# Reordering the first and last microseconds of an attention and feed-forward kernel: an earlier load, output tiles between the last contexts, adds on GpSimd, the last two tiles by halves

## The chip, the cores and the metric

The kernel runs on one core of one Trainium2 chip. The metric is the device time of one execution in microseconds (us), the median over several executions. PE is TensorE, DVE is VectorE, ACT is ScalarE, POOL is GpSimd, SP is SyncE, whose queue issues most DMAs. The *span* is the length of the profiled execution on the core, 1.75 to 1.92 us less than the device time.

## The reference

```python
# x: 2048 x 640; 32 heads of 192; only the last W = 512 keys are used
xn = layernorm(x)
q  = (xn @ wq) per head;  k, v = the last 512 rows of the caches
o  = softmax(q k^T * 192**-0.5) v          # per head
s  = concat(o) @ wo                        # 2048 x 640
g  = silu((silu(xn @ w_gate) * (xn @ w_up)) @ w_down)
return x + s * g
```

## The kernel before

The kernel handles the 2048 rows as 16 tiles of 128 rows. A context is one block of 512 rows (four tiles) of one pair of heads. It starts with the layernorm of the first four tiles and the gate and up products of the feed-forward part, then the rest of that part, then sixteen head pairs of attention. `sacc` collects x + g * (partial sum of `o @ wo`), `g2` holds g. In the last head pair the final sum of each tile is `PSUM * g2 + sacc`, a multiply on VectorE out of PSUM and an add of two SBUF tensors.

The start (cut):

```python
        load_x(0)
        load_x(1, nc.scalar)
        for cs in (slice(0, 1), slice(1, 3), slice(3, NC)):     # NC = 5 chunks of 128
            for eng, w_sb, w in ((nc.sync, wg_sb, B_w_gate), (nc.scalar, wu_sb, B_w_up)):
                ...                                             # a slice of each weight
        load_x(2)
        load_x(3)
        ...
        keep_warm(11)                       # matmuls on zeros
        def ready(t):                       # transposes on PE, then copies to SBUF
            ln_transpose(t)                 # five transposes
            rows = slice(t * P, (t + 1) * P)
            n = NC if t else 3
            nc.scalar.copy(xnT[:, 0:n, rows], tps[t][:, 0:n, :])
            if n < NC:
                nc.vector.tensor_copy(out=xnT[:, n:NC, rows], in_=tps[t][:, n:NC, :])
        ...
        keep_warm(3)
        for t in range(4):                  # t = 0 goes chunk by chunk, others bank by bank
            ...                             # after 3/5 of tile t's matmuls: normalise and ready(t + 1)
```

The end (cut). `pv` computes a half context, `wo_last` an output tile. Contexts 2 and 3 also take in the previous head pair there (`late`), so a tile of theirs has 12 matmuls and a tile of contexts 0 and 1 has 6. `sc_tile()` and `mm_tile()` give PSUM buffers out of two pools of two buffers each.

```python
    def wo_last(b, qt, eng):
        ...
        split = b == NB - 1 and qt == 3                # the last tile by halves
        sc = None if split else sc_tile()
        ...                                            # 6 or 12 matmuls
        if not split:
            nc.vector.tensor_tensor(s_f, sc, g2[t], ALU.mult)
            eng.tensor_tensor(ob, s_f, sacc[t], ALU.add)
        stores.append((t, ob))
    ...
    for b in range(NB - 1):
        for q2 in range(2):
            pv(i + b, q2)
    for q2 in range(2):
        wo_last(0, 2 * q2, G); wo_last(0, 2 * q2 + 1, G)
        pv(i + 3, q2)
    for qt in range(4):
        wo_last(1, qt, G)
        store(3)
        wo_last(2, qt, V if qt % 2 else G)
        transpose_o(i + 3, qt)                         # three PE transposes and a ScalarE copy
    for qt in range(4):
        store(2)
        wo_last(3, qt, V if qt else G)
    store(0)
```

The softmax here doesn't subtract the row's maximum and nothing guards it: scores larger than these inputs give would overflow.

## Time and profile before

| before | |
|---|---|
| time, median of 3 | 929.49 us (929.24 to 929.5) |
| span | 927.8 us |
| PE busy | 919.5 us (99%) |
| first matmul of the last head pair's `pv` ("the mark") | 890.91 us |
| last vector add ends | 924.97 us |

"The mark": between the start and this matmul PE never waits for long, so the time of the mark tells what the start cost, and times counted from it tell what the end cost.

From the page (engine, busy us, share, number of instructions; then the chain that ended last):

```profile
span 927.8 us, 18795 instructions
PE 919.5 (99%) x8009; PEld 578.7 (62%) x8025; DVE 579.4 (62%) x846; ACT 475.5 (51%) x849; POOL 65.0 (7%) x57
...
PE 98%; DMA 1%; DVE 1%; issue 0%; DVEq 0%
```

PE bounds everything but the edges. The start, from the timeline (start us, length us, engine, line, operation, output<-inputs, shapes, count, in brackets the engine's idle time before it and what ended it):

```profile
8.09 0.44 PE L262 MATMUL tp<-ident,xn 128*128 128x128 bf16 x5
...
8.37 0.22 PE L274 MATMUL sc<-xnT,wg_sb 128*128 128x128 bf16 x1
...
8.79 0.89 DVE L228 BATCH_NORM_STATS2 stats<-x_t 128x6 f32<-128x320 bf16 x2 [0.90 <-DMA x_t<-in_A_x_dram]
...
10.48 0.45 DVE L251 TENSOR_SCALAR xn<-x_t,mv,rstd 128x640 bf16<-128x640 bf16 x1
...
10.98 0.45 PE L262 MATMUL tp<-ident,xn 128*128 128x128 bf16 x5 [0.67 <-DVE xn L251]
```

VectorE waited for the third x tile until 8.79, so PE had its third tile to transpose only at 10.98, after 0.67 us of idle. The end, same view:

```profile
890.91 1.51 PE L461 MATMUL mm<-V_p,p_t 128*128 128x193 bf16 x16
...
907.57 0.33 PE L495 MATMUL trp<-ident,O_b 128*128 128x128 bf16 x3
...
907.73 0.98 PE L508 MATMUL sc<-wo_p,OT_b 128*128 128x320 bf16 x6
907.84 0.82 DVE L551 TENSOR_TENSOR s_f<-sc,g_76 128x640 f32<-128x640 f32 x1 [0.80 <-PE sc L508]
...
908.72 0.57 PE L508 MATMUL sc<-wo_p,OT_l 128*128 128x320 bf16 x3
...
916.26 1.55 POOL L554 TENSOR_TENSOR x_r<-s_f,sacc 128x640 bf16<-128x640 f32 x1
...
917.02 1.47 DVE L554 TENSOR_TENSOR ob<-s_f,sacc 128x640 bf16<-128x640 f32 x1
...
919.59 0.82 DVE L551 TENSOR_TENSOR s_f<-sc,g_76 128x640 f32<-128x640 f32 x1 [0.37 <-PE sc L508]
...
920.45 1.07 DVE L554 TENSOR_TENSOR ob<-s_f,sacc 128x640 bf16<-128x640 f32 x1
...
922.17 0.57 PE L508 MATMUL mm<-wo_p,OT_b 128*128 128x320 bf16 x3
...
924.48 0.49 DVE L549 TENSOR_TENSOR ob<-s_f,sacc 128x320 bf16<-128x320 f32 x1
```

A matmul of 320 columns takes PE 0.136 us in a row (12 in 1.63 us), but its printed length includes the modelled way through the array. So the six from 907.73 leave PE free at 908.55, and PE starts again at 908.72: 0.17 us lost. The same loss comes twice more, at 911.49 and 914.26.

### The profile page before, as it was taken

The page shows a single profiled execution, that of the slowest core. Times are in us where ns is not written, and L with a number is a line of the kernel's source. Part 1 is how long each engine was busy: PE and PEld are TensorE (multiplying, and loading weights), DVE is VectorE, ACT ScalarE, POOL GpSimd, SP SyncE. Part 2 cuts the span into 40 slices and gives each one's busy share as a digit, 9 for nine tenths or more (in the row PEclk, how much of TensorE's full clock was granted, in tenths as well). Part 3 has the DMA queues.
Part 4 walks back from the last instruction along what each step waited for, and adds up shares of the span by engine and source line. Part 5 has one row for each costly group of instructions (what it writes and reads, how often), then busy time and mean ns, then how long its engine had stood idle before and what let it go on. Part 6 is the DMA issues. An engine that isn't in the chain of part 4 may idle for free.

```text
span 927.8 us, 18795 instructions
## 1 busy us (share of the span) xinstructions
PE 919.5 (99%) x8009; PEld 578.7 (62%) x8025; DVE 579.4 (62%) x846; ACT 475.5 (51%) x849; POOL 65.0 (7%) x57
## 2 busy tenths in 40 slices
PE   9999999999999999999999999999999999999997
PEld 5455556574848474757575757575656666666675
DVE  6433331467676767676766666676767676767656
ACT  4222222556465656565655555555555555656561
POOL 0000000000000000000000000000000000003975
PEclk9999999999999999999999999999999999999999
DMA  9321510053525343433434342525252516262623
GB/s 300 69 54 34 114 35 1 1 86 79 102 62 92 72 86 77 79 86 74 90 72 92 65 99 59 105 53 111 41 122 40 124 35 129 35 144 59 147 59 107
DMA packets 240148, 76.34 MB, mean 82 GB/s; under 512 B 221120, under 2 KB 240064, under 8 KB 240064
## 3 DMA queue, kind: packets, MB, share of 16 engines
q1 hardware_dynamic: 239152, 74.40, 37.7%
q8 instruction: 63, 1.03, 0.5%
q10 hardware_dynamic: 912, 0.74, 0.3%
q14 instruction: 21, 0.17, 0.1%
HBM read 39.45 MB, written 2.62 MB: 45 GB/s over the span
## 4 chain that ended last, share of the span: by engine, by line
PE 98%; DMA 1%; DVE 1%; issue 0%; DVEq 0%
PE sc L508 22%; PE mm L425 22%; PE mm L461 18%; PE sc L439 18%; PE sc L274 10%; PE mm L296 6%; DMA x_t<-in_A_x_dram 1%; PE sc L461 1%; PE mm L274 0%; PE mm L309 0%; DVE s_f L551 0%; PE mm L439 0%; DVE stats L228 0%; DVE ob L549 0%; DVE s_f L548 0%
## 5 line engine op out<-in xcount | busy, mean ns | idle before, releaser
L443 ACT ACTIVATE p_t<-sc 128x1024 bf16<-128x1024 f32 x254 | 253.0, 1022 | 136.6 <-PE sc L439 136.6
L430 DVE TENSOR_REDUCE qT<-mm 128x512 bf16<-128x1024 f32 x189 | 231.2, 1223 | 104.0 <-PE mm L425 101.6
L478 ACT ACTIVATE O_b<-mm,r 128x192 bf16<-128x192 f32 x484 | 164.1, 421 | 175.5 <-DVE r L467 96.9
L425 PE MATMUL mm<-xnT,wq_p 64*128 64x512 bf16 x1890 | 235.0, 376 | 0.0
L508 PE MATMUL sc<-wo_p,OT_b 128*128 128x320 bf16 x1482 | 223.4, 299 | 0.0
L523 DVE TENSOR_TENSOR sacc<-sacc,sc 128x640 f32<-128x640 f32 x216 | 176.7, 821 | 60.9 <-PE sc L508 60.9
L439 PE MATMUL sc<-qT,khat 64*128 64x512 bf16 x1524 | 195.5, 376 | 0.0
L461 PE MATMUL mm<-V_p,p_t 128*128 128x193 bf16 x1984 | 185.8, 246 | 0.0
L461 PEld LDWEIGHTS <-p_t 128*128 128x128 bf16 x2048 | 173.0, 97 | 14.9 <-issue 7.0
L508 PEld LDWEIGHTS <-OT_b 128*128 128x128 bf16 x1488 | 143.5, 98 | 47.3
L425 PEld LDWEIGHTS <-wq_p 64*128 64x128 bf16 x1890 | 90.7, 94 | 112.4 <-issue 4.2
L439 PEld LDWEIGHTS <-khat 64*128 64x128 bf16 x1536 | 74.8, 94 | 91.0
L282 DVE TENSOR_TENSOR hT<-sc,sg 128x512 bf16<-128x512 f32 x46 | 31.6, 690 | 85.2 <-ACT sg L281 85.1
L526 POOL TENSOR_TENSOR sacc<-sacc,g_76 128x640 f32<-128x640 f32 x16 | 22.1, 1402 | 757.8 <-ACT O_b L478 757.8
L467 DVE RECIPROCAL r<-mm 128x4 f32<-128x4 f32 x124 | 22.7, 183 | 73.0 <-PE mm L461 68.9
L281 ACT ACTIVATE sg<-sc 128x512 bf16<-128x512 f32 x46 | 27.3, 596 | 72.4 <-PE sc L274 72.4
L274 PE MATMUL sc<-xnT,wg_sb 128*128 128x512 bf16 (+1 forms) x248 | 58.4, 353 | 0.7
L274 PE MATMUL sc<-xnT,wu_sb 128*128 128x512 bf16 (+1 forms) x259 | 59.0, 354 | 0.1
L296 PE MATMUL mm<-wd_sb,hT 128*128 128x320 bf16 x384 | 56.6, 299 | 0.0
L296 PEld LDWEIGHTS <-hT 128*128 128x128 bf16 x384 | 37.6, 98 | 18.9
L274 PEld LDWEIGHTS <-wu_sb 128*128 128x128 bf16 x285 | 26.3, 98 | 26.8 <-issue 0.2
L274 PEld LDWEIGHTS <-wg_sb 128*128 128x128 bf16 x285 | 26.4, 98 | 23.1 <-issue 0.2
(63 smaller groups left out, 250.9 us busy)
## 6 DMA issues: line engine op xcount, KB each, us to landing
wo_p<-in_A_wo_dram SPq DMA_DIRECT2D x16, 480.0 KB, 4.3
K_p<-in_A_k_cache_dram SPq DMA_DIRECT2D x32, 192.0 KB, 3.3
V_p<-in_A_v_cache_dram SPq DMA_DIRECT2D x32, 192.0 KB, 3.1
wq_p<-in_A_wq_dram SPq DMA_DIRECT2D x64, 80.0 KB, 3.1
wq_p<-in_A_wq_dram SPq DMA_DIRECT2D x16, 160.0 KB, 3.3
x_r<-in_A_x_dram SPq DMA_DIRECT2D x16, 160.0 KB, 3.6
x_t<-in_A_x_dram SPq DMA_DIRECT2D x14, 160.0 KB, 3.1
wd_sb<-in_B_w_down_dram SPq DMA_DIRECT2D x1, 1920.0 KB, 12.1
```

The costliest lines, as they stand in the source:

```text
L274: nc.tensor.matmul(out, w_sb[:, c, f * P : (f + 1) * P], xnT[:, c, qc], start=(c == 0), stop=(c == NC - 1),)
L281: nc.scalar.activation(sg[:], g, ACT.Silu)
L282: nc.vector.tensor_tensor(hTs[b][:, f, :], u, sg[:], ALU.mult)
L296: nc.tensor.matmul(dn[:, 0:HD], hTs[b][:, f, ti * P : (ti + 1) * P], wd_sb[:, f, cols], start=(f == 0), stop=(f == NF - 1),)
L425: nc.tensor.matmul(q_ps[:, h, :], pairs[pr]["wq"][r, c, j * P : (j + 1) * P], xnT[r, c, b * 512 : (b + 1) * 512], start=(c == 0), stop=(c ...
L430: nc.vector.reduce_sum(qTs[i][:, j, :], q_ps[:, :, :].rearrange("p h n -> p n h"), axis=AX.X)
L439: nc.tensor.matmul(sc[:, h, :], khat[r, j, ks], qT[r, j, :], start=(j == 0), stop=(j == 2))
L443: nc.scalar.activation(p_t[:, :, :], sc[:, :, :], ACT.Exp, scale=scale)
L461: nc.tensor.matmul(acc[:, k, h * 256 : h * 256 + Dh + 1], Ps[i][kc][:, h, qt * P : (qt + 1) * P], V_p[:, kc, h, 0 : Dh + 1], start=(kc == ...
L478: nc.scalar.activation(O_b[:, qt, h, :], a_k[:, h, 0:Dh], ACT.Copy, scale=r[:, k, h, :])
L508: nc.tensor.matmul(ps, OTs[i][:, 3 * qt + j, :], pairs[i // NB]["wo"][:, j, n * HD : (n + 1) * HD], start=(first and j == 0), stop=(end an ...
L523: nc.vector.tensor_tensor(s_t, s_t, sc[:, :, 0:HD], ALU.add)
```

## The change

Its intent: take the last PE transposes away (the DMA transposes instead), interleave output tiles with the last half contexts so that what they wait for is there, leave nearly all adds to GpSimd, and finish the last two tiles by halves with small stores. At the start, load the third x tile ahead of the last weight slices and let the first tile's chunks 0 and 1 go ahead. The diff, cut to its core:

```diff
         for cs in (slice(0, 1), slice(1, 3), slice(3, NC)):
+            if cs.stop == NC:
+                load_x(2)
             for eng, w_sb, w in ((nc.sync, wg_sb, B_w_gate), (nc.scalar, wu_sb, B_w_up)):
...
-        load_x(2)
         load_x(3)
...
-            n = NC if t else 3
+            n = NC if t else 2
...
-        ln_stats(1, lambda: ln_apply(0))
+        ln_stats(1, lambda: ln_apply(0, (slice(0, 2 * P), slice(2 * P, D))))
...
-        if (pr == last and b < NB - 1) or i == 0:
+        if pr == last or i == 0:
             nc.sync.dma_start_transpose(
...
+    def wo_end():
+        i = NS - 1
+        obs = [finp.tile([P, D], bf, name="ob", bufs=4) for k in range(2)]
+        s_fs = [finp.tile([P, 2, HD], f32, name="s_f", bufs=4) for k in range(2)]
+        for qt, n, mm in ((3, 0, mm_tile), (2, 0, mm_tile), (2, 1, sc_tile), (3, 1, sc_tile)):
+            t, cols = T - 4 + qt, slice(n * HD, (n + 1) * HD)
+            ob, s_f = obs[qt - 2], s_fs[qt - 2]
+            ps = mm()[:, 0, 0:HD]
+            wo_sum(ps, i, qt, n)
+            nc.vector.tensor_tensor(s_f[:, n, :], ps, g2[:, t, cols], ALU.mult)
+            nc.vector.tensor_tensor(ob[:, cols], s_f[:, n, :], sacc[:, t, cols], ALU.add)
+            (nc.scalar if n else nc.sync).dma_start(...)
...
+    work = [(0, 0), (0, 1), (1, 0), (1, 1), (2, 0)]
+    for b, q2 in work:
+        pv(i + b, q2)
+    for b, q2, more in ((0, 0, (2, 1)), (0, 1, (3, 0)), (1, 0, (3, 1)), (1, 1, None)):
+        for k in range(2):
+            wo_last(b, 2 * q2 + k, G)
+        if more:
+            pv(i + more[0], more[1])
+    for b in (2, 3):
+        for qt in range(4 if b < 3 else 2):
+            store(3)
+            wo_last(b, qt, V if (b, qt) == (3, 1) else G)
     store(0)
+    wo_end()
```

More of the change, by code (lines that the diff above doesn't have):

```diff
@@ L243, in ln_sqrt, with ln_apply @@
             )
-        def ln_apply(t):
+        def ln_apply(t, parts=(slice(0, D),)):
             b, ti = divmod(t, 4)
@@ L250, in ln_apply @@
                 nc.vector.reciprocal(rstd[:, t : t + 1], rstd[:, t : t + 1])
-            nc.vector.tensor_scalar(
-                xns[t][:], x_t.pop(t)[:], mv[:, ti, 0:1], rstd[:, ti : ti + 1],
-                op0=ALU.subtract, op1=ALU.mult,
-            )
+            for cols in parts:
+                nc.vector.tensor_scalar(
+                    xns[t][:, cols], x_t[t][:, cols], mv[:, ti, 0:1], rstd[:, ti : ti + 1],
+                    op0=ALU.subtract, op1=ALU.mult,
+                )
         tps = {}
@@ L453, in pv @@
         O_b, OT_b = Obs[i], OTs[i]
-        alone = i < 2 or (pr == last and b < NB - 1)
+        alone = i < 2 or (pr == last and 2 * b + q2 < 5)
         acc = sc_tile() if alone and q2 and b < 2 else mm_tile()
@@ L489, in pv @@
             )
-    def transpose_o(i, qt):
-        trp = psum.tile([P, 3, P], bf, name="trp", tag="mm")
-        o_f = Obs[i][:, qt, :, :].rearrange("p h d -> p (h d)")
-        for j in range(3):
-            nc.tensor.transpose(trp[:, j, :], o_f[:, j * P : (j + 1) * P], ident[:])
-        nc.scalar.copy(OTs[i][:, 3 * qt : 3 * qt + 3, :], trp[:, :, :])
     def load_xr(t):
@@ L537, in wo_last @@
         ob = xrs[t] if b < 2 else finp.tile([P, D], bf, name="ob", bufs=4)
-        s_f = finp.tile([P, 2, HD], f32, name="s_f", bufs=3)
-        halves = [slice(n * HD, (n + 1) * HD) for n in range(2)]
-        split = b == NB - 1 and qt == 3
-        sc = None if split else sc_tile()
-        ps = [(mm_tile()[:, 0, :] if split else sc[:, n, :])[:, 0:HD] for n in range(2)]
-        for n, cols in enumerate(halves):
-            if late(i):
-                wo_mm(ps[n], i - NB, qt, n, end=False)
-            wo_mm(ps[n], i, qt, n, first=not late(i))
-            if split:
-                nc.vector.tensor_tensor(s_f[:, n, :], ps[n], g2[:, t, cols], ALU.mult)
-                nc.vector.tensor_tensor(ob[:, cols], s_f[:, n, :], sacc[:, t, cols], ALU.add)
@@ L550, in wo_last @@
-        if not split:
-            nc.vector.tensor_tensor(
-                s_f[:], sc[:, :, 0:HD], g2[:, t, :].rearrange("p (n d) -> p n d", n=2), ALU.mult
-            )
-            eng.tensor_tensor(
-                ob[:], s_f[:].rearrange("p n d -> p (n d)"), sacc[:, t, :], ALU.add
-            )
-        stores.append((t, ob))
+        s_f = finp.tile([P, 2, HD], f32, name="s_f", bufs=4)
+        sc = sc_tile()
+        for n in range(2):
+            wo_sum(sc[:, n, 0:HD], i, qt, n)
+        nc.vector.tensor_tensor(
+            s_f[:], sc[:, :, 0:HD], g2[:, t, :].rearrange("p (n d) -> p n d", n=2), ALU.mult
+        )
@@ new lines, in wo_last, with wo_sum @@
+        eng.tensor_tensor(ob[:], s_f[:].rearrange("p n d -> p (n d)"), sacc[:, t, :], ALU.add)
+        stores.append((t, ob))
+    def wo_sum(ps, i, qt, n):
+        if late(i):
+            wo_mm(ps, i - NB, qt, n, end=False)
+        wo_mm(ps, i, qt, n, first=not late(i))
+    def wo_end():
[9 more added lines that the diff above has]
+            nc.vector.tensor_tensor(ob[:, cols], s_f[:, n, :], sacc[:, t, cols], ALU.add)
+            (nc.scalar if n else nc.sync).dma_start(
+                out=out2[t * P : (t + 1) * P, cols], in_=ob[:, cols]
+            )
@@ L603 @@
     V, G = nc.vector, nc.gpsimd
-    for b in range(NB - 1):
-        for q2 in range(2):
-            pv(i + b, q2)
-    for q2 in range(2):
-        wo_last(0, 2 * q2, G)
-        wo_last(0, 2 * q2 + 1, G)
-        pv(i + 3, q2)
-    for qt in range(4):
-        wo_last(1, qt, G)
-        store(3)
-        wo_last(2, qt, V if qt % 2 else G)
-        transpose_o(i + 3, qt)
-    for qt in range(4):
-        store(2)
-        wo_last(3, qt, V if qt else G)
+    work = [(0, 0), (0, 1), (1, 0), (1, 1), (2, 0)]
[10 more added lines that the diff above has]
+            wo_last(b, qt, V if (b, qt) == (3, 1) else G)
     store(0)
+    wo_end()
 _INS = ['A_x', 'A_k_cache', 'A_v_cache', 'A_wq', 'A_wo', 'B_x', 'B_w_gate', 'B_w_up', 'B_w_down']
```

## The prediction

> **What bounds the kernel.** The page gives PE busy 919.5 of 927.8 us, and the chain of waits is 98% PE. So only three things can pay: less PE work, less PE idle at the start, and a shorter end after PE's last matmul. The view of waits at the start shows one long PE idle, 0.67 us until 10.98 us, for the third normalised x tile, whose load (issued at 3.42) landed at 8.76. The timeline of the end shows PE's last matmuls ending near 922.7, VectorE until 924.97, then a 160 KB store (1.8 us to landing) and the program's closing at 927.8.
>
> **End.**
> (a) The last context's 12 PE transposes go (0.17 us for three: 0.68 us). The DMA transposes in their place land 2.8 us after issue and are wanted later than that, so PE should not wait for them.
> (b) Before, groups of 12 matmuls there take 1.79 us three times where others take 1.63: PE waited for PSUM that VectorE, busy with whole adds (0.8 to 1.47 us), had not read. With GpSimd adding, VectorE has one 0.82 us multiply for each 1.63 us tile; some 0.48 us go. PE's last matmul then comes about 1.15 us sooner.
> (c) Not all of that arrives. GpSimd now has 13 adds of 1.51 us in a row, from about 900.1 to 919.7. The whole add left on VectorE (tile 13) reads two SBUF tensors; in this trace such adds took 1.47 and 1.07 us beside a GpSimd add, and ended 0.7 us after it. The Trainium skill, "SBUF — State Buffer", section "Who interferes with whom", states that a VectorE op with two SBUF inputs contends with GpSimd's reads and the loser blocks; the trace agrees. So that add ends near 920.4. Then come four half pairs (multiply and add) on VectorE, 0.93 us a pair. My estimate for the last add's end is 924.15 (before 924.97): gain 0.8 us. VectorE, not PE, bounds the last 3 us.
> (d) The last store is 80 KB, on the ACT queue: gain 0.1 us, since landing is mostly fixed time.
>
> **Start.** The third x tile is issued about 0.8 us earlier, ahead of the last gate-weight slice; landing estimated at 7.5 to 8. The gate slice then lands about where x did (8.7; before 8.35) and holds PE before chunk 3, so the 0.4 us that the split normalise and shorter first copy give the first matmul is lost again. The next limit is the fourth x tile (landing 9.25), whose first half of statistics stands before the third tile's normalise on VectorE. I put the third tile's transposes at 10.4 to 10.7 instead of 10.98: gain 0.45 us. PE being full afterwards, this reaches the end.
>
> **Sum.** 929.49 - 0.45 - 0.8 - 0.1 = 928.1 us, range 927.3 to 928.9. Faster by over 2%: 0.01; within 2%: 0.98; slower by over 2%: 0.01.
>
> **What would show it.** First real matmul near 6.6 (before 7.06), then PE idle for the gate slice; idle before the third tile's transposes shrinking to 0.1 to 0.3 us; no PE idle from 891 on; PE's last matmul 1.6 us sooner in all; GpSimd busy without a gap for 19.6 us; tile 13's add on VectorE stretched over 0.9 us; four half pairs back to back after it.
>
> **What would make it wrong.** The x tile landing late all the same (loads share the DMA engines) would leave the start unchanged; a later gate slice would make it slower. GpSimd adds slower than 1.51 us, or a store holding an output buffer, would push the last pairs back. If VectorE kept up with PE, the end would gain up to 1.2 us.

## The result

| | before | changed |
|---|---|---|
| time, median of 6 | 929.5 us (928.81 to 929.72) | 928.21 us (927.87 to 928.43) |
| span of the profiled run | 927.8 us | 926.3 us |
| the mark | 890.91 us | 890.42 us |
| start of PE's last group, from the mark | 31.26 us | 30.44 us |
| last add's end, from the mark | 34.06 us | 33.25 us |
| last add's end to the end of the span | 2.83 us | 2.63 us |

A ratio is the mean time of one kernel's fast runs over the mean of the other's in the same rounds, so it is not quite the ratio of these medians. For this pair it is 0.9987 (95% interval 0.9974 to 1.0): within 2%. The 1.5 us of the span divide into 0.49 (start), 0.81 (until the last add) and 0.20 (the store). The medians differ by 1.29 us here and, in the later rounds of after_again, by 1.87 us, so a tenth of a microsecond in a single pair of medians means nothing.

The page after, the lines that answer those of before:

```profile
span 926.3 us, 18776 instructions
PE 918.8 (99%) x7997; PEld 578.1 (62%) x8013; DVE 576.7 (62%) x846; ACT 474.0 (51%) x847; POOL 67.9 (7%) x59
...
POOL 2%; DMA 1%; DVE 0%; issue 0%; DVEq 0%; POOLq 0%
```

The chain that ended last no longer runs back along PE. It goes back through GpSimd's row of adds and breaks off there (its shares add up to a few per cent only), so it must not be read as "GpSimd bounds the kernel": it says which engine's queue the last microseconds hang on. The start after, from the timeline:

```profile
7.95 0.89 DVE L229 BATCH_NORM_STATS2 stats<-x_t 128x6 f32<-128x320 bf16 x2
...
8.21 0.44 PE L264 MATMUL tp<-ident,xn 128*128 128x128 bf16 x5
...
8.95 0.23 PE L276 MATMUL sc<-xnT,wg_sb 128*128 128x128 bf16 x1 [0.30 <-DMA wg_sb<-in_B_w_gate_dram]
...
9.99 0.45 DVE L253 TENSOR_SCALAR xn<-x_t,mv,rstd 128x640 bf16<-128x640 bf16 x1
...
10.49 0.45 PE L264 MATMUL tp<-ident,xn 128*128 128x128 bf16 x5
```

The third x tile is there by 7.95, and the third tile's transposes come at 10.49 without idle: 0.49 us sooner, exactly what the mark moved. The price is at 8.95, where PE now waits for the gate slice that was pushed back. The end after, same view:

```profile
890.42 1.51 PE L463 MATMUL mm<-V_p,p_t 128*128 128x193 bf16 x16
...
899.53 12.04 POOL L540 TENSOR_TENSOR x_r<-s_f,sacc 128x640 bf16<-128x640 f32 x8 [5.39 <-DVE s_f L537]
...
906.26 1.79 PE L503 MATMUL sc<-wo_p,OT_b 128*128 128x320 bf16 x12
...
907.35 1.64 DVE L537 TENSOR_TENSOR s_f<-sc,g_76 128x640 f32<-128x640 f32 x2 [0.70 <-PE sc L503]
...
908.23 0.57 PE L503 MATMUL sc<-wo_p,OT_l 128*128 128x320 bf16 x3 [0.17 <-DVE s_f L537]
...
911.52 7.57 POOL L540 TENSOR_TENSOR ob<-s_f,sacc 128x640 bf16<-128x640 f32 x5
...
918.27 0.82 DVE L537 TENSOR_TENSOR s_f<-sc,g_76 128x640 f32<-128x640 f32 x1 [0.81 <-PE sc L503]
...
919.13 0.83 DVE L540 TENSOR_TENSOR ob<-s_f,sacc 128x640 bf16<-128x640 f32 x1
...
920.86 0.57 PE L503 MATMUL sc<-wo_p,OT_b 128*128 128x320 bf16 x3
...
923.18 0.49 DVE L559 TENSOR_TENSOR ob<-s_f,sacc 128x320 bf16<-128x320 f32 x1
```

Three things are to be seen. The twelve matmuls from 906.26 leave PE free at 907.89 (12 times 0.136 us), but it starts again only at 908.23, when the first multiply of the pair is done: a new wait of 0.34 us (0.17 by the modelled ends). GpSimd's 13 adds stand in one row from 899.53 to 919.09. And tile 13's add on VectorE starts at 919.13, just as both its multiply (918.27 + 0.82) and GpSimd's row end.

### The profile page after: what moved, and what is told of

The parts are those of the page before. It is cut to its first block, busy times and chain, and to the rows that moved or that the text cites. A ratio compares the mean times of both kernels' runs of the same rounds, so it can differ in the third digit from the quotient of the medians.

```text
span 926.3 us, 18776 instructions
## 1 busy us (share of the span) xinstructions
PE 918.8 (99%) x7997; PEld 578.1 (62%) x8013; DVE 576.7 (62%) x846; ACT 474.0 (51%) x847; POOL 67.9 (7%) x59
```

## The experiments

Eleven runs; all gave the right result. All were timed in five rounds, beside runs of the kernel before in the same rounds on the same chip. Since the effects are tenths of a microsecond and the times of one kernel in the same rounds scatter by 0.4 to 1.4 us, the verdicts rest on the mark and on times counted from it; the medians only point the same way. One profile is one execution, though, and the mark itself scatters with the landing of the first loads. The part after the mark does not: 34.06 to 34.08 us in all five profiles with the old end, 33.24 to 33.25 in all three with the new one.

| run | median us | before, same rounds | mark us | last add after the mark us |
|---|---|---|---|---|
| start_only | 929.1 | 929.61 | 890.33 | 34.07 |
| load_only | 929.23 | 929.61 | 891.24 | 34.08 |
| load_only_again | 929.15 | 929.74 | 890.48 | 34.07 |
| split_only | 929.83 | 929.96 | 891.46 | 34.06 |
| end_only | 928.3 | 929.61 | 891.39 | 33.24 |
| mm_tile | 928.01 | 929.61 | 890.46 | 33.08 |
| mm_relief | 928.19 | 929.74 | 890.57 | 33.06 |
| mm_half | 927.36 | 929.74 | 890.11 | 32.28 |
| mm_relief_half | 927.31 | 929.74 | 890.61 | 32.30 |
| after_again | 928.09 | 929.96 | 890.33 | 33.25 |
| mm_half_again | 927.11 | 929.96 | 890.70 | 32.27 |

(Runs with the same time of before shared their rounds and their chip.) Against before, every run is within 2%: the ratios go from 0.997 to 1.0001. For the four runs of the start alone the 95% interval of the ratio includes 1, so what the start is worth is read from the marks. Ten profiles have the earlier load, and nine of them have the mark between 890.11 and 890.70 (load_only, disturbed, at 891.24); the three without it have 890.91, 891.39 and 891.46.

### Is the gain made at the start or at the end? start_only and end_only

The edit of start_only is the kernel before with the first three hunks of the diff; end_only is the changed kernel with those hunks taken back:

```diff
 # start_only, against before (end_only is the reverse of this, against the changed kernel)
+            if cs.stop == NC:
+                load_x(2)
...
-        load_x(2)
...
-            n = NC if t else 3
+            n = NC if t else 2
...
-        ln_stats(1, lambda: ln_apply(0))
+        ln_stats(1, lambda: ln_apply(0, (slice(0, 2 * P), slice(2 * P, D))))
```

> The kernel before with the three edits of the start alone (third x tile loaded ahead of the last gate slice, first normalise in two parts, first copy of two chunks). My theory, parts that add: the start is worth 0.49 us (the matmuls of the attention's last stage begin at 890.42 instead of 890.91) and the end keeps its old shape, so the span is 927.3 and the time 929.0. Rival, the end alone makes the gain: no change from before (span 927.8).

> The changed kernel with the start put back. Theory: 0.81 us less until the last add and 0.2 us less for the smaller last store, span 926.8, time 928.5; the start shows 0.67 us of PE idle before the third tile's transposes, as before. Rival (start and end are not independent, a common wait hides one): span 927.3 or more.

start_only: mark at 890.33, old end (34.07), span 927.2, median 0.51 us under before. end_only: new end (33.24, closing 2.67 us), median 1.31 us under before. Its profiled span was 927.3, which is what I had named for the rival. But the excess lies before the mark: this execution had the old start with a late load (third tile's transposes at 11.47 after 0.75 us of idle, mark 891.39). So the two parts show no influence on each other: the old end takes as long after the new start, and the new end as long after the old start. The rival falls on the numbers after the mark. The single span was the wrong test; I should have named times from the mark.

### Which edit of the start? load_only, load_only_again, split_only

load_only has the moved `load_x(2)` alone, load_only_again is the same program, split_only has the two other hunks alone:

```diff
 # split_only, against before
-            n = NC if t else 3
+            n = NC if t else 2
-        ln_stats(1, lambda: ln_apply(0))
+        ln_stats(1, lambda: ln_apply(0, (slice(0, 2 * P), slice(2 * P, D))))
```

> The kernel before with the earlier load of the third x tile alone. Theory: the gate slice, landing near 8.95 us, is what the start waits for, so the split normalise and the shorter first copy are worth nothing and this run has all 0.49 us of the start (third tile's transposes near 10.49 us, span 927.3). Rival, the split helps: transposes 0.1 to 0.4 us later than 10.49, span 927.4 to 927.7.

> The run with the earlier load alone, once more, since its profile fell on an execution whose weight slices landed late (PE waited 0.64 us for the second up slice, which no other run shows). Theory (split worth nothing): last stage's matmuls start at 890.4 to 890.5 when the gate slice lands near 8.95, as with the split. Rival (split is worth 0.1 us or more): 890.55 or later, and the median over the rounds above that of the run with all three start edits (929.10) by as much.

> The kernel before with the split normalise and the shorter first copy, without the earlier load. Theory: worth nothing alone as well; the first transposes wait for the warm-up matmuls (5.9 us) and the copy waits for the fifth transpose whatever its own width, so the first real matmul stays at 7.05 to 7.2 us, the third tile's transposes wait for its load (near 11 us) and the last stage's matmuls start at 890.9 to 891.4, as before; median within 0.2 us of before. Rival (the split makes the first matmul 0.4 us earlier, as I predicted, and this reaches the end): first matmul near 6.65, start at 890.5.

load_only's profile fell on an execution in which the loads came late. PE waited 0.64 us for the second up slice, and its five times scatter from 928.63 to 930.02. So that profile decided nothing, and I ran it again. The repeat shows what the theory asks for:

```profile
8.09 0.89 DVE L229 BATCH_NORM_STATS2 stats<-x_t 128x6 f32<-128x320 bf16 x2
...
9.02 0.23 PE L275 MATMUL sc<-xnT,wg_sb 128*128 128x128 bf16 x1 [0.15 <-DMA wg_sb<-in_B_w_gate_dram]
...
10.55 0.45 PE L263 MATMUL tp<-ident,xn 128*128 128x128 bf16 x5
```

(load_only_again, timeline.) PE waits for the gate slice at 9.02, the third tile follows at 10.55, the mark is 890.48, among the marks with the split (890.11 to 890.70). The median is 929.15 against 929.1 with all three edits.

split_only has a median 0.13 us under before, with a ratio of 1.0001. Here I was wrong in one point: the first real matmul came at 6.86 us (before 7.06), not at 7.05 or later. So the split can make it sooner. But nothing comes of it: PE then waited 0.99 us for an up slice (this profile again had late loads) and the third tile's transposes came at 11.53. The split was worth nothing measurable in these runs, alone or on top of the load. In the changed kernel's own profile the first matmul came at 7.10 even with the split, for two reasons that can be read there: the first transposes start at 5.90, when the warm-up matmuls end, though the first part of the normalise is done sooner; and the copy of two chunks starts at 6.65, when the fifth transpose is through. In the built program that copy waits on a semaphore that only the fifth transpose raises.

### What holds the new end? mm_tile

The new wait of 0.34 us stands where three output tiles follow each other in a pool of two PSUM buffers, the middle one short. The edit puts the third one into the other pool:

```diff
-        sc = sc_tile()
+        sc = mm_tile() if (b, qt) == (2, 0) else sc_tile()
```

> The changed kernel with the first output tile of the third context in a PSUM buffer of the other pool. Theory A (two limits at once): PE's new wait of 0.34 us there goes and PE's last matmul comes 0.34 us sooner, but GpSimd's 13 adds still end near 919.1 us, so VectorE's whole add, ready at 918.8, is held until then and ends 0.7 us later; the four half pairs move by 0 to 0.05 us and the span stays at 926.2 to 926.3. Rival B (PE alone sets the end): span 0.34 us shorter, 925.95.

```profile
890.46 1.51 PE L463 MATMUL mm<-V_p,p_t 128*128 128x193 bf16 x16
...
907.93 0.57 PE L503 MATMUL mm<-wo_p,OT_l 128*128 128x320 bf16 x3
...
911.62 7.53 POOL L540 TENSOR_TENSOR ob<-s_f,sacc 128x640 bf16<-128x640 f32 x5
...
918.84 0.99 DVE L540 TENSOR_TENSOR ob<-s_f,sacc 128x640 bf16<-128x640 f32 x1
...
920.57 0.57 PE L503 MATMUL sc<-wo_p,OT_b 128*128 128x320 bf16 x3
```

(mm_tile, timeline.) PE goes on at 907.93 without a gap, and its last group starts 30.11 us after the mark instead of 30.44: the 0.34 us are the PSUM buffer's, shown. But the last add ends only 0.17 us sooner (33.08 instead of 33.25). VectorE's add is now ready at 918.84 while GpSimd's row ends at 919.15; it stretches to 0.99 us and ends 0.68 us after GpSimd. Theory A named 0 to 0.05 us and rival B 0.34; the truth lies between. The mechanism of A is there (the add ran up against GpSimd's row), but I counted the wait too dear: after such a wait VectorE's next operation starts 0.60 us after GpSimd is done (919.75 after 919.15), not 0.75, which is what an add that is not held takes from its own start to the next operation (919.13 to 919.88 in the changed kernel).

### Relieving GpSimd: mm_relief

```diff
 # on top of mm_tile
-            wo_last(b, qt, V if (b, qt) == (3, 1) else G)
+            wo_last(b, qt, V if (b, qt) in ((2, 1), (3, 1)) else G)
```

> The run with the other PSUM pool, and the add of the third context's second tile moved from GpSimd to VectorE, so GpSimd has 12 adds. If GpSimd's queue and PE limit the end together (theory A), both limits are now moved: GpSimd ends 0.8 to 1.5 us before the whole add of tile 13, which starts 0.05 us after its multiply and takes 0.75 us unblocked, and the last add ends 0.33 us sooner than in the changed kernel, counted from the start of the last stage's matmuls (32.92 instead of 33.25 us). Risk named beforehand: GpSimd's adds stand back to back, and VectorE's add may not get the port between them, but wait for several; then PE stops for PSUM and the end is not earlier than 33.08.

```profile
911.67 1.55 POOL L540 TENSOR_TENSOR ob<-s_f,sacc 128x640 bf16<-128x640 f32 x1
...
912.43 1.47 DVE L540 TENSOR_TENSOR ob<-s_f,sacc 128x640 bf16<-128x640 f32 x1
...
913.82 0.81 DVE L537 TENSOR_TENSOR s_f<-sc,g 128x640 f32<-128x640 f32 x1
...
914.71 4.53 POOL L540 TENSOR_TENSOR ob<-s_f,sacc 128x640 bf16<-128x640 f32 x3 [1.50 <-DVE s_f L537]
```

(mm_relief, timeline.) The theory fell: the last add ends 33.06 us after the mark, against 33.08. The add on VectorE waited for GpSimd's and took 1.47 us. The next multiply waited behind it, so GpSimd had nothing to add and sat idle for 1.50 us, until 914.71, as long as one of its own adds. The trace of before had already shown it: GpSimd idle for 1.50 us until 913.27 and for 1.49 us until 919.30, each time after a whole add on VectorE that it had held up. It ends 28.67 us after the mark (914.71 + 4.53 - 890.57) with 12 adds, and ended 28.69 us after it with 13. The feared case, VectorE not getting in between adds that stand back to back, wasn't met either: GpSimd's queue was empty behind the add it collided with.

### Taking adds from VectorE after the last whole tile: mm_half and mm_relief_half

```diff
 # wo_end, on top of mm_tile (mm_half) or of mm_relief (mm_relief_half)
             nc.vector.tensor_tensor(s_f[:, n, :], ps, g2[:, t, cols], ALU.mult)
-            nc.vector.tensor_tensor(ob[:, cols], s_f[:, n, :], sacc[:, t, cols], ALU.add)
+            # n == 0: add on nc.gpsimd; n == 1: both adds on nc.vector after the fourth multiply
```

> The run with the other PSUM pool, and the two first-half adds of the last pair of tiles moved to GpSimd, the two second-half adds after all four multiplies on VectorE. Theory: after tile 13's add VectorE alone bounds the end (eight operations of about 0.46 us), so taking two away gains 0.7 us after the run with the other PSUM pool (last add's end at about 32.4 us from the start of the last stage's matmuls instead of 33.08); time about 927.3. Rival (PE and the stores bound the end): under 0.2 us.

> All three edits. If the gains add, last add's end at about 32.1 us from the start of the last stage's matmuls, time about 927.0: 1.2 us under the changed kernel. If PE's last matmul (30.1 us by its start) is what is left, the end can't come before about 31.9.

```profile
918.49 0.99 DVE L540 TENSOR_TENSOR ob<-s_f,sacc 128x640 bf16<-128x640 f32 x1
...
919.40 0.88 DVE L558 TENSOR_TENSOR s_f<-mm,g 128x320 f32<-128x320 f32 x2
...
919.96 1.68 POOL L562 TENSOR_TENSOR ob<-s_f,sacc 128x320 bf16<-128x320 f32 x2 [1.16 <-DVE s_f L558]
...
920.20 1.11 DVE L558 TENSOR_TENSOR s_f<-sc,g 128x320 f32<-128x320 f32 x2
920.21 0.57 PE L503 MATMUL sc<-wo_p,OT_b 128*128 128x320 bf16 x3
...
921.23 1.16 DVE L562 TENSOR_TENSOR ob<-s_f,sacc 128x320 bf16<-128x320 f32 x2
```

(mm_half, timeline.) The multiplies, which read PSUM and one SBUF tensor, run beside GpSimd's half adds at their usual pace; VectorE's two adds are held until GpSimd is done at 921.64 and end at 922.39. From the mark that is 32.28 us: 0.80 us less than mm_tile (0.7 expected). PE's last group is where it was (30.10). So VectorE's row of eight operations was what bound the last microseconds, as predicted, and the rival falls. mm_relief_half (32.30) adds nothing, as mm_relief had added nothing.

### The version to keep: mm_half_again beside after_again

> The changed kernel once more, on the same chip and in the same rounds as the best version: 928.2 us; last stage's matmuls from 890.3 to 890.6, last add's end 33.25 us after that.

> The best version (other PSUM pool for one tile, two half adds on GpSimd) once more beside the changed kernel: 0.8 to 1.0 us under it (927.3), last add's end 32.3 us after the last stage's first matmul.

On one chip, in the same rounds: 928.09 us for the changed kernel (33.25 after the mark once more) and 927.11 us for mm_half (32.27), against 929.96 us for before. The mean of mm_half's five times over the mean of the changed kernel's (927.15 over 928.06) is 0.9990. All five of its times (926.82 to 927.55) lie below all five of the changed kernel's (927.73 to 928.54). Its ratio to before is 0.997 (0.9956 to 0.9983). So it is faster than the changed kernel by about one thousandth and than the kernel before by about three.

## Why the prediction was right or wrong

The time was right: 928.1 predicted, 928.21 measured, inside the range, and "within 2%" as expected. The terms show how far this was understanding:

- **"(a) The last context's 12 PE transposes go ... 0.68 us"**: right. Four gaps of 0.165 us went (907.57 to 907.73 is one of them), 0.66 us, and no wait for the DMA transposes took their place.
- **"(b) ... PE waited for PSUM that VectorE, busy with whole adds ... had not read ... some 0.48 us go"**: the loss was there, but cause and size were wrong. The trace shows VectorE idle for 0.80, 0.97 and 0.20 us before the three multiplies that PE waited for. What bounds is the rotation of two PSUM buffers: tile k + 2 can start only when tile k's multiply is done, 1.15 us after PE has issued the whole of tile k (907.57 to 908.72 before: 0.27 us until the multiply starts, 0.82 us for the multiply, 0.06 us until PE starts). PE has only tile k + 1 to fill this time. Before, that was a short tile and three transposes, 0.98 us: loss 0.17, three times, 0.50 us in all. Changed, it is a short tile without transposes, 0.82 us, once: loss 0.34. Net gain 0.16 us instead of 0.48. For the changed kernel's wait, mm_tile shows that the buffer, not an add, holds PE; for the three losses before, this is read from the trace and no run tested it. So PE's last group came 0.82 us sooner (31.26 to 30.44), not 1.15.
- **"(c) ... gain 0.8 us. VectorE, not PE, bounds the last 3 us"**: the sum was right (0.81), partly by luck. What happened is plainer than the sum: tile 13's multiply waits for PE in both kernels (919.59 before, 918.27 changed) and comes 0.83 us sooner from the mark, which is PE's gain. From there to the last add VectorE takes 5.38 us before and 5.40 changed. The add that is no longer stretched lets the next operation start 0.25 us sooner (0.75 instead of 1.00 us after its own start), and taking tile 14 by halves, four operations instead of two, costs 0.27 us. So by these traces the second tile by halves gained nothing on VectorE as far as the last add goes; no run tested it alone. Against the prediction: GpSimd's row is as predicted (899.53 to 919.09, 19.56 us for 13 adds). Tile 13's add was not stretched: because of PE's new wait, it became ready only when GpSimd was done. In mm_tile, where PE runs as I had assumed, the add is stretched (0.99 us) and the gain is 0.98 us (34.06 less 33.08). So I was 0.18 us too cautious on the collision and did not see the 0.34 us wait, which cost 0.17 us at the end, and the two cancelled. That VectorE bounds the last stretch is shown by mm_half. The rule that I cited from the Trainium skill, "SBUF — State Buffer", section "Who interferes with whom", agrees with all traces: whole adds of two SBUF inputs that ran into one of GpSimd's took 0.92 to 1.50 us instead of 0.82 (the three of before and those of mm_tile and mm_relief all ended 0.68 us after the GpSimd add), while multiplies with one SBUF input kept their 0.82.
- **"(d) The last store is 80 KB ... gain 0.1 us"**: the 80 KB stores landed 1.6 us after issue, the 160 KB ones 1.8; from the last add to the end the profile shows 0.20 us less. Half of this was counted. An estimate agrees: the fit in the Trainium skill, "DMA: Bandwidth & Descriptors", section "Anatomy of one DMA — SWDGE (gpsimd) path", has a part that grows as bytes over 436 GB/s, which makes 0.19 us for 80 KB. That fit is for DMAs issued by GpSimd, and these stores are issued by SyncE and ScalarE, so the measured 0.2 us decides.
- **"Start ... gain 0.45 us"**: the size was right (0.49). First matmul "near 6.6": wrong, 7.10; a step without consequence, as load_only_again shows. Gate slice at 8.7: it came at 8.95, since its issue also waited 0.4 us for the semaphore of an earlier x load (the view of waits). "The next limit is the fourth x tile": half right. Its wait is there on VectorE (0.32 us, until 9.40) and the normalise ends at 10.44, but PE, held up by the gate slice, is free only at 10.47 (10.19 and five matmuls of 0.055 us), so PE has no idle before the third tile's transposes, where I had named 0.1 to 0.3 us. The Trainium skill, "DMA: Bandwidth & Descriptors", section "Issuing engines are not separate DMA queues", says that all loads end on the same 16 DMA engines whichever queue issues them, so moving one tile forward should put another load back. The trace agrees as far as it goes: the 16 engines are busy throughout from 6 to 12 us, at 350 GB/s before and 347 after. But it does not show this as the reason for the later slice. From issue to landing the slice took 5.6 us before and 5.4 changed, the third x tile 5.3 and 5.2. So both landings moved with their issues on SyncE's queue: the slice's from 2.7 to 3.5 us, the tile's from 3.42 to 2.70.

What stays open: how much of the start's scatter (marks from 890.11 to 891.46) is the code's and how much the memory's. The late up slices of load_only and split_only were seen in one profile each, and the repeat of load_only did not show it. The end was run only as a whole: the missing PE transposes, the new order, the adds moved to GpSimd and the second tile by halves were not run one by one, so their shares (0.66 us for the transposes above all) are read from the traces.

## What to carry to other kernels

With two PSUM buffers in rotation, work out for each tile: the delay from when PE has issued its last matmul to when its buffer can be written again, less the PE time of the one tile that stands between; what is left is PE idle, even when the evacuating engine is nearly idle. Where two engines share the closing work, look at two things before moving an operation to the other one: whether it will run into an operation of the first engine that holds it up, and whether what is queued behind it feeds the first engine. In mm_relief both were so, and moving the add gained nothing. Count the start and the end of a kernel from a mark in the trace between them; one whole span mixes the luck of the first loads with the effect that is being tested.

## What the Trainium skill lacked or had wrong

- "SBUF — State Buffer", section "Who interferes with whom": nothing wrong was found. It lacks the price to expect when VectorE waits: here a 128x640 add of 0.82 us took 0.92 to 1.50 us and ended 0.68 us after GpSimd's add (mm_tile), so less than its full length was left to do by then. It also lacks the second-order effect: in mm_relief the held add delayed the next multiply, and GpSimd itself then sat idle for 1.50 us.
- "DMA: Bandwidth & Descriptors", section "Anatomy of one DMA — SWDGE (gpsimd) path": its fit gives a fixed part of about 2.0 us and is for DMAs issued by GpSimd. The stores here, issued by SyncE and ScalarE, landed in 1.6 us (80 KB) and 1.8 us (160 KB) in all, under that fixed part; the page has no such fit for these queues.
- No page that I used gives the evacuation rule above with a number: 1.15 us from when PE has issued the whole of a tile to the first matmul that reuses its buffer, for a multiply of 0.82 us.
